# Chunks 6 and 7 of a retention layer computed in halves of 64 tokens, with their k and v loaded head by head

## The chip, the core and the metric

One core of one Trainium2 chip runs the whole program in a single launch. The core has a matrix engine (TensorE, "PE" in the profile, whose weight loads are listed apart as "PEld"), a vector engine (VectorE, "DVE"), a scalar engine (ScalarE, "ACT"), GpSimd ("POOL") and SyncE ("SP"). In this kernel SP issues every DMA, one after the other, from one queue. The metric is the device time of one execution in microseconds; lower is better.

## The reference

Two layers follow each other. The first is a recurrent retention over q, k and v of shape (4 batches, 8 heads, 768 tokens, 64); the second is a feed-forward layer with a squared ReLU over the 4 x 768 = 3072 tokens of width 512.

```python
gamma = 1.0 - 2.0 ** (-5.0 - np.arange(H))
scale = 1.0 / np.sqrt(D)
for t in range(S):
    state = gamma[None, :, None, None] * state + np.einsum('bhd,bhe->bhde', k[:, :, t], v[:, :, t])
    y[:, :, t] = scale * np.einsum('bhd,bhde->bhe', q[:, :, t], state)
...
x = y.transpose(0, 2, 1, 3).reshape(B * S, H * D)
h = np.maximum(x @ w_in, 0.0)      # w_in: 512 x 2048
out = h * h @ w_out                # w_out: 2048 x 512
```

## The kernel before

**Chunks.** The tokens are cut into 24 chunks of 128 (six for each batch): chunks 0 to 5 are batch 0, 6 to 11 batch 1, and so on. In a chunk the recurrence is replaced by matrix products: scores of q against k, masked to the causal half, times v, plus q times the state that the chunks before have left. The powers of gamma are multiplied into q and k beforehand. Heads are taken in four pairs.

**Three ways to compute a chunk.** Chunks 0 to 3 are done in pairs before the main loop (`..._pair` functions). From there on there are two ways, and `PACK_FROM` (L25) says where the second begins:

- Whole chunks (`attend`, L916): `scale_q` and `scale_kv` (DVE for q and k, POOL for v) make bf16 copies, `transpose_q` (L360) and `transpose_k` (L374) transpose them on PE, `scores` (L396) multiplies 128 tokens by 128 tokens, `state` (L420) adds k times v to the state in PSUM (`c_ps`) and copies it to a block-diagonal SBUF tile (`s_bd`), and `outputs` (L465) makes `y` and copies it to `xt`, the input of the feed-forward layer. q, k and v come by `load_q` (L84, 512 KB for two chunks) and `load_kv` (L102, 256 KB for k and 256 KB for v of one chunk).
- Halves of 64 tokens (`attend2`, L928): the two heads of a pair stand on the two halves of the partitions. `scale_k2` (L618, DVE, two instructions), `cast_v2` (L631, POOL: a plain copy `v2` and two instructions for the block-diagonal `v_bd`), `transpose_k2` (L642) and `dma_transpose_q` (L388), which transpose by DMA, `scores2` (L651), `state2` (L678, once for each half; its result goes to `s_bd` first on ACT, L697, and then on DVE, L698), `outputs2` (L700; its copy to `xt` on ACT is L724). k and v come by `batch_loads` (L120): eight DMAs for each part of a batch, one for each head, each of them 64 partitions wide. The tile that they fill comes from the `stage` pool, which the weights have used before.

**Feed-forward.** `BLOCKS` (L18) groups the chunks: block 0 has chunks 0 to 3, each block after it has two. `ffn_pieces` (L786) yields after every piece of PE work. A piece is 16 products with `w_in` (L757, 128 columns) or four with `w_out` (L815, 512 columns) around here. Block 1 (chunks 4 and 5) has pieces 33 to 48: 33 to 40 the first product, 33 to 36 of chunk 4 and 37 to 40 of chunk 5, 41 to 48 the second. Block 2 (chunks 6 and 7) has pieces 49 to 64 in the same way: 49 to 52 need `xt` of chunk 6, 53 to 56 that of chunk 7. Block 3 (chunks 8 and 9) begins with piece 65.

**Order of the work.** There is no scheduler. `put(place, ...)` writes by hand after which piece each step of the attention is issued, and every engine takes its instructions in that order. A place therefore fixes the order on each engine and in SP's queue, not a time: an engine that has nothing to wait for runs ahead of PE. `done` (L961) is the place of `outputs2` for each chunk done by halves, and `attend2` puts the chunk's `state2` and `scores2` at fixed distances ahead of it. `places` (L971) spreads the single DMAs of `batch_loads`.

Lines that matter most here:

```python
put(max(d - 6, before), state2, m, 0)
put(d - 5, scores2, m)
put(d - 3, state2, m, 1)
put(d, outputs2, m)
```

## Time and profile before

| | |
|---|---|
| median of 3 runs | 213.44 us (213.25 to 213.58) |
| the profiled execution | 215.1 us, its core's span 213.3 us |
| granted TensorE clock, mean | 0.998 |
| DVE, ACT and POOL busy | 63%, 55% and 27% of the span |
| DMA moved | 40.18 MB in 92,727 packets, 68,512 of them under 512 B |
| L757 and L815, the feed-forward products | 90.6 us and 89.6 us of PE's busy time |
| L132, a load of 128 KB | 8 for k, 5.8 us from issue to landing; 8 for v, 5.1 us |
| L108, a load of 256 KB | 4 for k, 6.1 us; 4 for v, 6.5 us |
| L645, transposition of k by DMA | 16, 3.8 us |
| L391, transposition of q by DMA | 8, 3.4 us |

The profile is one execution. An engine's busy time is a union of its instructions; PE's matmuls are pipelined and overlap, so the distance from one start to the next is the better measure of what a matmul costs. A wait is put down to the last semaphore that it needed. Positions such as "at 60.72 us" are counted from the start of the span.

### The profile page before, as it was taken

The page shows a single profiled execution, that of the slowest core. Times are in us where ns is not written, and L with a number is a line of the kernel's source. Part 1 is how long each engine was busy: PE and PEld are TensorE (multiplying, and loading weights), DVE is VectorE, ACT ScalarE, POOL GpSimd, SP SyncE. Part 2 cuts the span into 40 slices and gives each one's busy share as a digit, 9 for nine tenths or more (in the row PEclk, how much of TensorE's full clock was granted, in tenths as well). Part 3 has the DMA queues.
Part 4 walks back from the last instruction along what each step waited for, and adds up shares of the span by engine and source line. Part 5 has one row for each costly group of instructions (what it writes and reads, how often), then busy time and mean ns, then how long its engine had stood idle before and what let it go on. Part 6 is the DMA issues. An engine that isn't in the chain of part 4 may idle for free.

```text
span 213.3 us, 5243 instructions
## 1 busy us (share of the span) xinstructions
PE 205.2 (96%) x2117; PEld 141.4 (66%) x2117; DVE 134.7 (63%) x263; ACT 117.0 (55%) x220; POOL 57.9 (27%) x114
## 2 busy tenths in 40 slices
PE   5798999999999999999999999999999999999994
PEld 1467744457965984884875875874965965965853
DVE  4677787235798997396495596595694793640410
ACT  8345887158953763662663663652753754643631
POOL 5232458223102523142230343052130433000000
PEclk9999999999999999999999999999999999999999
DMA  5999999999999997969978998959988451701102
GB/s 163 292 318 383 383 384 252 285 242 293 247 160 175 259 167 140 254 111 231 189 124 152 271 166 205 242 105 190 239 150 211 103 98 49 101 0 52 49 0 98
DMA packets 92727, 40.18 MB, mean 188 GB/s; under 512 B 68512, under 2 KB 86176, under 8 KB 92704
## 3 DMA queue, kind: packets, MB, share of 16 engines
q1 hardware_dynamic: 92704, 39.86, 83.1%
q8 instruction: 16, 0.26, 0.5%
q14 instruction: 7, 0.06, 0.1%
HBM read 27.26 MB, written 6.29 MB: 157 GB/s over the span
## 4 chain that ended last, share of the span: by engine, by line
PE 78%; DVE 8%; SPq 5%; DMA 4%; ACT 3%; issue 1%; ACTq 0%; DVEq 0%
PE psf L815 34%; PE psf L757 33%; SPq L132 4%; DMA kn<-in_k_dram 3%; DVE ks_bdp L623 2%; DVE h L737 2%; DMA stage<-in_v_dram 2%; PE y L717 2%; PE y L710 2%; PE st L661 2%; PE c_ps L688 1%; PE y L316 1%; PE c_ps L565 1%; DVE pt L548 1%; PE psf L524 1%
## 5 line engine op out<-in xcount | busy, mean ns | idle before, releaser
L757 PE MATMUL psf<-xt,w_in_bf 128*128 128x256 bf16 (+2 forms) x880 | 90.6, 259 | 0.2 <-ACT xt L488 0.2
L815 PE MATMUL psf<-w_out_bf,h 128*128 128x512 bf16 (+2 forms) x400 | 89.6, 371 | 0.0
L757 PEld LDWEIGHTS <-w_in_bf 128*128 128x128 bf16 x880 | 71.1, 98 | 11.6 <-issue 0.3
L766 ACT ACTIVATE h<-psf 128x512 bf16<-128x512 f32 x96 | 57.1, 597 | 22.2 <-PE psf L757 19.4
L815 PEld LDWEIGHTS <-h 128*128 128x128 bf16 x400 | 36.0, 98 | 35.7 <-DVE h L737 1.0
L737 DVE TENSOR_TENSOR h<-h 128x512 bf16<-128x512 bf16 x96 | 45.1, 492 | 17.8 <-ACT h L766 17.2
L698 DVE CAST s_bd<-c_ps 64x256 bf16<-64x256 f32 x29 | 12.4, 427 | 31.1 <-ACT s_bd L697 30.8
L637 POOL CAST v_bd<-stage 64x512 bf16<-64x512 f32 x32 | 23.2, 726 | 28.1 <-PE y L717 27.1
L825 ACT ACTIVATE osb<-psf 128x512 f32<-128x512 f32 (+2 forms) x25 | 14.5, 580 | 28.8 <-PE psf L815 28.8
L634 POOL CAST v<-stage 128x512 bf16<-128x512 f32 x16 | 11.3, 705 | 61.7 <-DMA stage<-in_v_dram 28.8
L623 DVE TENSOR_TENSOR ks_bdp<-stage,kf 64x512 bf16<-64x512 f32 x32 | 24.9, 779 | 0.6
L724 ACT ACTIVATE xt<-y 128x512 bf16<-128x512 f32 x16 | 11.9, 741 | 13.5 <-PE y L717 13.5
L335 DVE TENSOR_TENSOR qs<-qn,qf 128x512 bf16<-128x512 f32 x22 | 15.4, 709 | 2.3 <-DMA qn<-in_q_dram 2.0
L697 ACT ACTIVATE s_bd<-c_ps 64x256 bf16<-64x256 f32 x29 | 10.6, 367 | 10.3 <-PE c_ps L688 8.1
L411 DVE TENSOR_TENSOR pt<-st,cmask 128x512 bf16<-128x512 f32 x8 | 5.5, 689 | 10.1 <-PE st L404 10.1
L668 DVE TENSOR_TENSOR pt<-st,cmask 128x512 bf16<-128x512 f32 x16 | 11.1, 691 | 0.5
L304 POOL CAST w_out_bf<-stage 128x512 bf16<-128x512 f32 x12 | 8.3, 724 | 5.3 <-DMA stage<-in_moe_w_out_dram 5.3
L688 PEld LDWEIGHTS <-ks_bdp 128*128 128x128 bf16 x116 | 7.2, 98 | 3.4 <-issue 0.4
L717 PE MATMUL y<-pt,v_bd 128*128 128x64 bf16 x128 | 9.4, 193 | 0.0
L710 PE MATMUL y<-qT,s_bd 128*128 128x64 bf16 x120 | 9.1, 193 | 0.0
L710 PEld LDWEIGHTS <-s_bd 128*128 128x128 bf16 x120 | 8.2, 98 | 1.1
L717 PEld LDWEIGHTS <-v_bd 128*128 128x128 bf16 x128 | 8.1, 98 | 1.2
(99 smaller groups left out, 141.9 us busy)
## 6 DMA issues: line engine op xcount, KB each, us to landing
qn<-in_q_dram SPq DMA_DIRECT2D x12, 512.0 KB, 5.0
out_dram<-osb SPq DMA_DIRECT2D x23, 256.0 KB, 3.8
stage<-in_moe_w_out_dram SPq DMA_DIRECT2D x4, 1024.0 KB, 8.0
stage<-in_moe_w_in_dram SPq DMA_DIRECT2D x3, 1024.0 KB, 11.7
stage<-in_k_dram SPq DMA_DIRECT2D x32, 96.0 KB, 3.6
stage<-in_v_dram SPq DMA_DIRECT2D x32, 96.0 KB, 3.3
kn<-in_k_dram SPq DMA_DIRECT2D x2, 512.0 KB, 6.8
vn<-in_v_dram SPq DMA_DIRECT2D x2, 512.0 KB, 7.5
```

The source lines that it names most:

```text
L335: engine.tensor_tensor(out=out, in0=by, in1=table[:, :, None].to_broadcast([P, H, D]), op=ALU.mult)
L623: nc.vector.tensor_tensor(out=ks[rows, :, hh, :].rearrange("s (u p) d -> s u p d", u=2), in0=kn[rows], in1=kf2[rows, i, :, :, None].to_bro ...
L637: nc.gpsimd.tensor_copy(v_bd[rows, :, hh, :].rearrange("s (u p) d -> s u p d", u=2), vn[rows])
L698: nc.vector.tensor_copy(s_bd[halves[1], :, 1, :], c[halves[1]])
L710: nc.tensor.matmul(yv, lhsT=s_bds[(2 * m + u - 1) % 3][:, p], rhs=half_of(a["qT"], p, u), start=True, stop=False,)
L717: nc.tensor.matmul(yv, lhsT=a["v_bd"][:, u * NPAIR + p], rhs=a["pt"][:, u * NPAIR + p, :].rearrange("s (r t) -> s r t", r=2), start=not inter,
L724: nc.scalar.activation(xts[tb][:, :, off : off + C].rearrange("e p (s r) -> e p r s", r=2), y[:], AF.Copy,)
L737: nc.vector.tensor_mul(hv, hv, hv)
L757: nc.tensor.matmul(hp, lhsT=w_in_bf[g][:, cb, fq * 128 : (fq + 1) * 128], rhs=xts[tb][:, cb, cols], start=(cb == 0), stop=(cb == NCB - 1),)
L766: nc.scalar.activation(hv, hp[:], AF.Relu)
L815: nc.tensor.matmul(op[:], lhsT=h_of(tb, f)[:, 0, j * C : (j + 1) * C], rhs=w_out_bf[g][:, fq, cols], start=(f == 0), stop=(f == NFB - 1),)
L825: nc.scalar.activation(osb[:, cols], op[:], AF.Copy)
```

## The change

`PACK_FROM` goes from 8 to 6, so chunks 6 and 7 are computed in halves too. What follows from it:

- Their k and v are no longer loaded by `load_kv`. `batch_loads` now takes a list of widths: for batch 1 `[2, 4]`, that is eight DMAs of 64 KB for chunks 6 and 7 and eight of 128 KB for chunks 8 to 11; for the other batches `[3, 3]` as before. k of 6 and 7 is issued at places 13 and 14. v of 6 and 7 is issued at places 31, 32, 35 and 36, two at each. The DMA that transposes q of chunks 6 and 7 is put at place 31 and that of k of chunk 6 at place 34. k and v of 8 to 11 move from places 30 to 37 to places 38 to 45.
- `outputs2` of chunks 6, 7, 8 and 9 stands at places 47, 52, 59 and 63 (before: `outputs` of 6 and 7 at 42 and 49, `outputs2` of 8 and 9 at 57 and 62).
- The constants and the zeroing for the halves are made earlier. The loads of q for 6 and 8 move by one place, and those of batch 2 by two or three.
- `state` serves chunk 4 alone now, and loses its form for the batches after the first.

```diff
-PACK_FROM = 8
+PACK_FROM = 6
...
-        for w in range(0, NCH - i, size):
+        for w, size in zip(np.cumsum([0] + sizes).tolist(), sizes):
...
-    for m, place in ((5, 10), (6, 14), (7, 18)):
-        put(place, load, m)
+    put(10, load, 5)
+    put(13, load_q, 6)
...
-    attend(6, 30, (33, 35, 37, 39, 42))
-    attend(7, None, (40, 42, 44, 46, 49))
-    put(34, pack_constants)
-    for j, t in enumerate([s_bds[2]] + ks_bd2s + v_bd2s):
+    put(24, pack_constants)
+    for t, place in zip(ks_bd2s + [s_bds[2]] + v_bd2s, (22, 24, 26, 34, 36)):
         for hh in range(2):
-            put(35 + 2 * j + hh, zero_off_diagonal, t, hh)
-
-    put(29, load_q, 8)
+            put(place + hh, zero_off_diagonal, t, hh)
+
+    put(30, load_q, 8)
     put(41, load_q, 10)
-    done = [57, 62] + [70 + 8 * j for j in range(14)]
+    done = [47, 52, 59, 63] + [70 + 8 * j for j in range(14)]
 
     ahead = {
-        8: (36, 40, 44, 46, 48), 9: (0, 0, 49, 51, 53), 10: (50, 54, 55, 57, 58), 11: (0, 0, 60, 63, 63)
+        6: (29, 31, 33, 34, 41), 7: (0, 0, 36, 38, 44), 8: (42, 45, 48, 50, 49), 9: (0, 0, 52, 54, 54),
+        10: (50, 55, 57, 59, 60), 11: (0, 0, 61, 63, 64),
     }
...
     places = {
-        (8, "k"): [30 + j // 2 for j in range(8)],
-        (8, "v"): [34 + j // 2 for j in range(8)],
-        (12, "k"): [47, 48, 49, 50, 52, 53, 55, 56] + [74 + j for j in range(8)],
-        (12, "v"): [58, 59, 60, 61, 62, 64, 65, 66] + [82 + j for j in range(8)],
+        (6, "k"): [13 + j // 4 for j in range(8)] + [38 + j // 2 for j in range(8)],
+        (6, "v"): [31, 31, 32, 32, 35, 35, 36, 36] + [42 + j // 2 for j in range(8)],
+        (12, "k"): [50, 51, 53, 54, 55, 56, 57, 58] + [74 + j for j in range(8)],
+        (12, "v"): [60, 61, 62, 64, 65, 66, 67, 68] + [82 + j for j in range(8)],
...
-        loads = batch_loads(m, name, 4 if m == 8 else 3)
+        loads = batch_loads(m, name, [2, 4] if m == 6 else [3, 3])
```

In `ahead` the five numbers are the places of `scale_q`, `dma_transpose_q`, `scale_k2`, `transpose_k2` and `cast_v2`. The instructions as built: PE has eight matmuls fewer (2111 instead of 2119, branches counted), SP 15 DMAs more, POOL four casts more, DVE two instructions more, ACT three fewer. In SP's queue the order around the change is: q of 6 and 7, the eight k loads of 6 and 7, two stores of results, q of 8, a third store, the transposition of q of 6 and 7, two v loads, the fourth store, two v loads, the transposition of k of 6, four v loads, the transposition of k of 7, six k loads of 8 to 11, q of 10, two k loads, four v loads, a store, two v loads, the transposition of q of 8 and 9, two v loads.

More of the change, by code (lines that the diff above doesn't have):

```diff
@@ L118, in stage_tile, with batch_loads @@
         return t[:, 0:size]
-    def batch_loads(m, name, size):
+    def batch_loads(m, name, sizes):
         b, i = chunks[m]
@@ L426, in state @@
         if i == 0:
-            c_ps[0] = ps_c.tile([P, NPAIR, D], FP32, name="c_ps")
+            c_ps[0] = ps_c.tile([P, NPAIR, 2, D], FP32, name="c_ps")
         c = c_ps[0]
-        if b == 0:
-            for p in range(NPAIR):
-                nc.tensor.matmul(
-                    c[:, p],
-                    lhsT=a["ks"][:, 2 * p : 2 * p + 2, :],
-                    rhs=a["v_bd"][:, p, ::3, :],
-                    start=False,
-                    stop=True,
-                    skip_group_check=True,
-                )
-        else:
-            for p in range(NPAIR):
-                for hh, head in enumerate(halves):
-                    nc.tensor.matmul(
-                        c[head, p, :],
-                        lhsT=a["ks"][:, 2 * p + hh, :],
-                        rhs=a["v_bd"][:, p, 3 * hh, :],
-                        start=(i == 0 and p == 0),
-                        stop=True,
-                        skip_group_check=True,
-                    )
-        s_bd = s_bds[(2 * m + 1) % 3]
-        for hh, head in enumerate(halves):
-            of = c[head, :, hh, :] if b == 0 else c[head]
+        for p in range(NPAIR):
+            nc.tensor.matmul(
+                c[:, p],
+                lhsT=a["ks"][:, 2 * p : 2 * p + 2, :],
+                rhs=a["v_bd"][:, p, ::3, :],
+                start=(i == 0 and p == 0),
+                stop=True,
+                skip_group_check=True,
+            )
+        s_bd = s_bds[m % 2]
+        for hh in range(2):
+            rows = slice(64 * hh, 64 * (hh + 1))
             if hh < on_scalar:
-                nc.scalar.activation(s_bd[head, :, hh, :], of, AF.Copy)
+                nc.scalar.activation(s_bd[rows, :, hh, :], c[rows, :, hh, :], AF.Copy)
             else:
-                nc.vector.tensor_copy(s_bd[head, :, hh, :], of)
+                nc.vector.tensor_copy(s_bd[rows, :, hh, :], c[rows, :, hh, :])
     def xt_of(m):
@@ L473, in outputs @@
                     y[:, p, :],
-                    lhsT=s_bds[(2 * m - 1) % 3][:, p],
+                    lhsT=s_bds[(m - 1) % 2][:, p],
                     rhs=a["qT"][:, :, p, :],
```

## The prediction

> **What bounds the kernel now.** I read the page first (busy time, chain), then PE's timeline and SP's, then the landings of DMAs and the casts on POOL.

> ```profile
> PE 205.2 (96%) x2117; PEld 141.4 (66%) x2117; DVE 134.7 (63%) x263; ACT 117.0 (55%) x220; POOL 57.9 (27%) x114
> ```

> PE is busy for 205.2 of 213.3 us. Of the 8.1 us idle most lies in the first 20 us (PE busy for 15.5 of them) and in the last 13; between 30 and 200 us the timeline has three waits, of 0.19, 0.18 and 0.14 us. So the time is PE's work, and nearly every new wait of PE is added to it. PE's timeline where the change works, columns start, length, instruction, count:

> ```profile
> 59.82 1.07 PE L757 MATMUL psf<-xt,w_in_bf 128*128 128x128 bf16 x16
> 60.72 1.89 PE L815 MATMUL psf<-w_out_bf,h 128*128 128x512 bf16 x8
> 62.45 0.61 PE L480 MATMUL y<-pt,v_bd 128*128 128x128 bf16 x8
> 63.24 0.40 PE L378 MATMUL tp<-ident,ks 128*128 128x128 bf16 x4 [0.18 <-DVE ks L335]
> ...
> 79.06 0.28 PE L688 MATMUL c_ps<-v,ks_bdp 128*128 128x64 bf16 x4
> 79.18 0.40 PE L661 MATMUL st<-qT,kT 128*128 128x64 bf16 x8
> 79.41 1.89 PE L815 MATMUL psf<-w_out_bf,h 128*128 128x512 bf16 x8
> 81.44 0.28 PE L688 MATMUL c_ps<-v,ks_bdp 128*128 128x64 bf16 x4
> ```

> The reader takes start-to-start distances: a piece of 16 L757 costs 0.90 us, a piece of four L815 0.865 us, and place 40 is at 60.72. SP's queue is the other thing to see:

> ```profile
> 50.90 0.57 SPq L827 DMA_DIRECT2D out_dram<-osb  x1
> 51.52 1.30 SPq L132 DMA_DIRECT2D stage<-in_k_dram  x2
> 52.92 0.68 SPq L827 DMA_DIRECT2D out_dram<-osb  x1
> 53.65 3.60 SPq L132 DMA_DIRECT2D stage<-in_k_dram  x4
> 57.34 6.71 SPq L132 DMA_DIRECT2D stage<-in_v_dram  x8
> 64.16 1.70 SPq L391 DMA_TRANSPOSE qT<-qs  x1
> ```

> From 49 to 66 us SP issues without a gap, and one load takes it 0.63 us at least (median 0.65 for these eight v loads, some up to 1.4). What hangs on it:

> ```profile
> 67.71 0.89 POOL L634 CAST v<-stage 128x512 bf16<-128x512 f32 x1 [11.42 <-DMA stage<-in_v_dram]
> ```

> POOL has waited 11.42 us for the last of these loads. Today that is harmless: `state2` of chunk 8 needs this cast at 72.80 only.

> **PE's work.** Removed, by distances in PE's timeline: transposition of q of 6 and 7 0.45 (eight at 52.33); of k 0.22 and 0.23; scores with state 0.22 + 0.56 for each chunk (59.26 to 59.82 holds four scores and eight state products); outputs 0.79 for chunk 6 (62.45 to 63.24, the wait of 0.18 with it) and 0.67 for chunk 7. Sum 3.92 us. Added, from the same operations on later chunks: four states of 0.12, two scores of 0.23, outputs 0.46 (78.60 to 79.06) and 0.35 for a batch's first chunk (107.82 to 108.17). Sum 1.75. Net **-2.17 us**. A wait for `xt` of chunk 5 takes back 0.1, since only piece 36 is left between its `outputs` and piece 37. On DVE, ACT and POOL the differences hide: PE waits for none of their sums, only at the points below.

> **Hand-over of chunk 7 (B).** `outputs2` of chunk 7 is at place 52 and piece 53 reads its `xt` at once; before, three pieces lay between. After chunk 8's last output at 79.06 ACT starts the copy at 79.26 and takes 0.75, so PE stands still for **1.0 us** (up to 1.6 if a ReLU of 0.60 is ahead on ACT; not below 0.9, there is nothing to cover it).

> **State of chunk 9 (C).** Its two `state2` are now at places 59 and 60 with one piece between, 0.12 + 0.865 = 0.98 us from start to start. The second overwrites the PSUM that ACT and DVE copy, behind chunk 8's copy to `xt`. In the lines above the same pair is 2.38 us apart, of it the wait of 0.14. DVE came 0.7 us late there, behind squares of h; without them it would be 1.7. So PE waits 0.7 to 1.4; I take **1.1**, less today's 0.14.

> **v of chunk 6 (D).** `state2` of chunk 6 at place 41 needs `cast_v2`, and that all eight v loads. When does PE come? 60.72 less what is removed ahead of it (0.45 + 0.22 + 0.22 + 0.56 = 1.45), plus 0.1, plus piece 41: **60.2**. When does v come? Until the third store PE and SP run as now, so it issues at 50.90, when ACT has its result, and ends at 51.5. Then SP issues in turn, each with 0.04 between: transposition of q 1.32 (the q copy on DVE was done by 49.6), two loads 1.34, a store 0.6, two loads 1.34, transposition of k 1.3, three loads 2.0. The eighth starts at 59.5. From issue to landing v loads take

> ```profile
> stage<-in_v_dram SPq DMA_DIRECT2D x32, 96.0 KB, 3.3
> stage<-in_v_dram SPq DMA_DIRECT2D x8, 128.0 KB, 5.1
> ```

> No row has 64 KB. From below: 2.6, the shortest of any load between 45 and 110 us; from above: 5.1. I take 3.3, the nearest size. POOL started 0.3 after the landing (the load issued at 63.42 landed 4.0 later) and casts in 0.66 to 0.89: v2 is there at 63.8, from 62.8 (2.6 + 0.66 and no delay) to 65.8. PE waits **3.6 us** (2.6 to 5.6). Moving the k loads of 6 and 7 to places 13 and 14 costs nothing: eight of 0.67 take the 5.1 us that four loads take now (41.42 to 46.53), ahead of the first store at 47.54. Behind the waiting state stand all of PE's later pieces.

> [...] Here v of 6 and 7 costs SP 2.26 us now (1.25 at 42.45, 1.01 at 45.52) and 5.4 then. [...]

> **v of chunks 8 to 11 (E).** It stands behind all that: from 59.5, the eighth load 0.67, transposition of k of 7 1.33, six k loads 4.0, q 0.62, two k 1.34, four v 2.7, a store 0.6, two v 1.34, transposition of q 1.37, one v 0.67. The last load starts at 74.2, against 63.42 now. It lands 4.0 later, as the last one does now; POOL 0.3 and 0.89: **79.4**. From below (2.6 and 0.66): 77.5. From above: the twelve loads from 53.65 to 64.05 took 0.87 each, 0.2 more than 0.67; for 15 loads 3.0, so 82.4. PE comes to place 53 at 63.8 + 13.3 = 77.1. The 13.3 are the pieces 42 to 53, 0.865 or 0.894 each, 10.5 us; four states, two scores and two outputs, 1.75; and B. So PE waits another 2.3.

> **Sum.** From place 53 on, the run of before takes 213.3 - 74.93 = 138.4 us (74.93 is where piece 53 ends now, 73.81 + 0.23 + 0.89). Then come 0.35 for the state and score of chunk 8, which lay ahead of it, and C's 0.96: 139.7. 79.4 + 139.7 = 219.1 us of span. By terms: 213.3 - 2.17 + 0.1 + 3.6 + 1.0 + 2.3 + 0.96 = 219.1. The profiled execution's own time is 215.1 and its span 213.3; the median of the runs, 213.44, lies 0.14 above that span, so I predict **219.2 us**.

> **Rivals.**
> 1. Only v of 6 is late; SP's later loads land in time (E = 0). For it: in the stage from 69.5 the loads of 96 KB already took 3.3. Against it: fifteen loads, three more issues than now and the chain from the third store stand ahead of the last one. 77.1 + 139.7 = 216.8, so 216.9 us; with D at its lower end 215.9.
> 2. The other side, not slower: SP's queue keeps ahead of PE. It decides at 59.2 us, when the eighth load would have to have landed, and at 72.5 for the last one of chunks 8 to 11. Then place 53 is at 60.2 + 13.3 = 73.5, and 213.2 + 0.14 = 213.3 us; with B at 0.9 and C at 0.7, 212.8. For it: SP waits for nothing of PE but stores, and the DMAs have 0.5 MB less to fetch between 41 and 47 us. Against it: the third store ties the queue to ACT at 50.90, and the ten issues between it and the eighth load take 8.0 us.
> 3. The DMA engines are the bound, and loads come at 0.87: place 53 at 82.4, 222.2 us. For it: the DMA share is 9 of 10 or more from 20 to 70 us. Against it: that stage now holds fewer bytes.

> That the change doesn't do what it says is excluded by the order of the built instructions.

> **How the numbers follow.** Forecast 0.60 (its own range 217.2 to 221); rival 1 0.18; rival 3 0.14; rival 2 0.08. The range from 215.8 to 222.4 leaves out rival 2 and parts of the others' tails, some 0.17. About 0.2% is what a measurement of this kernel can tell from no change, so of rival 2's 0.08 half is within it and half faster (212.8 and less); all else is slower: 0.92.

> **What would show it.** PE waits at L688's `c_ps` for POOL's v2 cast near 60 and near 77 us, some 3.6 and 2.3 long; one of 1.0 for ACT's `xt` just ahead, near 75; one of about 1 for DVE's `s_bd` near 87. SP issues without a gap from 49 to 75, with the last v load of chunk 8 at 74. L757 and L815 keep their busy time. I am wrong if PE's waits between 55 and 90 us sum to under 4 us, if the waits name a kT or ks_bdp instead of v2, or if v loads land under 2 us.

## The result, and the profile after

The changed kernel takes 226.1 us (median of 4 runs, 224.63 to 226.69) where the kernel before takes 213.34 on the same chip: a ratio of 1.0577, 95% interval 1.0546 to 1.0608. It is slower, as forecast, but by 12.8 us instead of 5.8, and it lies above the range. The profiled execution took 226.39 us, its span 224.6.

First PE's busy time and granted clock (the 40 slices are 5.6 us each):

```profile
PE 206.2 (92%) x2087; PEld 142.4 (63%) x2109; DVE 133.6 (59%) x265; ACT 114.5 (51%) x217; POOL 59.3 (26%) x118
...
PEclk9999999999979976999999999999999999999999
```

and the clock row of before:

```profile
PEclk9999999999999999999999999999999999999999
```

PE has less to do and is still busy a microsecond longer. The clock row says why: in three slices, 62 to 67 and 79 to 90 us, the clock fell; in the profile of before it is at half only from 212.44 us on, behind PE's last product. PE's timeline shows where (start, length, instruction, count, and in brackets the wait ahead of it with what ended it):

```profile
63.85 0.28 PE L675 MATMUL c_ps<-v,ks_bdp 128*128 128x64 bf16 x4 [4.30 <-POOL v L621]
63.97 1.75 PE L802 MATMUL psf<-w_out_bf,h 128*128 128x512 bf16 x4
65.51 0.64 PE L648 MATMUL st<-qT,kT 128*128 128x64 bf16 x8
...
77.90 1.05 PE L744 MATMUL psf<-xt,w_in_bf 128*128 128x128 bf16 x16 [0.85 <-ACT xt L711]
83.19 0.37 PE L675 MATMUL c_ps<-v,ks_bdp 128*128 128x64 bf16 x4 [4.23 <-POOL v L621]
83.37 1.90 PE L744 MATMUL psf<-xt,w_in_bf 128*128 128x128 bf16 x16
...
93.57 0.28 PE L675 MATMUL c_ps<-v,ks_bdp 128*128 128x64 bf16 x4 [0.54 <-DVE s_bd L685]
```

All four waits that the forecast named are there, at the instructions and for the releasers that it named: D 4.30, B 0.85, E 4.23, C 0.54. These are idle times; from start to start, as the forecast counted, they are 4.46, 1.02, 4.40 and 0.70. (The lines are those of before less 13: L675 was L688, L621 was L634.) Behind D four products with `w_out` take 1.54 us from start to start, 63.97 to 65.51, where before they took 0.865. Behind E a piece of 16 products with `w_in` takes 1.69, 83.37 to 85.06, instead of 0.89. SP's queue, in which v comes:

```profile
51.01 2.41 SPq L391 DMA_TRANSPOSE qT<-qs  x1
53.51 1.27 SPq L132 DMA_DIRECT2D stage<-in_v_dram  x2
...
58.45 2.60 SPq L132 DMA_DIRECT2D stage<-in_v_dram  x4
61.16 1.26 SPq L632 DMA_TRANSPOSE kT<-ks_bdp  x1
62.46 4.64 SPq L132 DMA_DIRECT2D stage<-in_k_dram  x6
...
69.21 4.04 SPq L132 DMA_DIRECT2D stage<-in_v_dram  x4
...
77.49 2.38 SPq L132 DMA_DIRECT2D stage<-in_v_dram  x2
```

The eighth load of v of 6 and 7 starts at 60.43 (forecast 59.5), the last of v of 8 to 11 at 79.23 (forecast 74.2, before 63.42). Four 128 KB loads that were to take 2.7 us take 4.04, two take 2.38. POOL answers with its casts:

```profile
63.19 0.61 POOL L621 CAST v<-stage 128x512 bf16<-128x512 f32 x1 [17.63 <-DMA stage<-in_v_dram]
...
82.52 0.61 POOL L621 CAST v<-stage 128x512 bf16<-128x512 f32 x1 [15.60 <-DMA stage<-in_v_dram]
```

**Where the 11.3 us of span come from.** I compare both traces between two instructions that both have, the 65th product with `w_in` and the 400th from the last. That stretch takes 83.93 us before and 96.05 after, 12.12 more; ahead of it the profiled execution of before is 0.84 slower, behind it both are alike. The gaps between PE's instructions sum to 0.50 before and 10.58 after: +10.08. The rest is work, 83.42 and 85.47. In an execution without loads of v and of the later k (`no_kv_loads` below, clock 1.00) the same work takes 81.89. So PE's own work fell by 1.53, and the fallen clock added 85.47 - 81.89 = 3.58. -1.53 + 10.08 + 3.58 = 12.13.

What the DMAs did meanwhile, as busy time by stretch (PE, PEld, DVE, ACT and POOL with their counts, then the granted clock; the last two numbers are the busy share of the 16 DMA engines and GB/s), before:

```profile
42.00:53.00 11.00, 10.81 (x101) 6.92 (x100) 4.86 (x8) 6.97 (x14) 4.20 (x18) 1.00 1.25 265
53.00:63.00 10.00, 10.00 (x159) 8.80 (x156) 8.22 (x22) 7.23 (x13) 0.76 (x1) 1.00 1.14 212
63.00:73.00 10.00, 9.82 (x112) 6.79 (x111) 8.76 (x16) 5.33 (x9) 4.72 (x6) 1.00 1.10 222
```

and after:

```profile
42.00:53.00 11.00, 10.76 (x111) 7.39 (x111) 6.01 (x10) 7.05 (x13) 2.34 (x4) 1.00 0.81 190
53.00:63.00 10.00, 6.50 (x103) 5.85 (x102) 6.08 (x15) 4.52 (x8) 0.00 (x0) 1.00 0.98 195
63.00:73.00 10.00, 9.10 (x72) 4.75 (x73) 3.04 (x6) 2.22 (x6) 3.55 (x6) 0.83 0.92 183
73.00:83.00 10.00, 5.10 (x99) 4.89 (x96) 6.54 (x13) 4.45 (x8) 0.48 (x1) 0.91 1.19 188
```

From 42 to 73 us the DMAs move 265 x 11 + 212 x 10 + 222 x 10 = 7.3 MB before and 5.9 MB after. A queue that issues one load of 64 KB in 0.66 us feeds 99 GB/s; the 1.4 MB that are missing come later, when the engines are busier again (share 1.19).

### The profile page after: what moved, and what is told of

The parts are those of the page before. It is cut to its first block, busy times and chain, and to the rows that moved or that the text cites. A ratio compares the mean times of both kernels' runs of the same rounds, so it can differ in the third digit from the quotient of the medians.

```text
span 224.6 us, 5233 instructions
## 1 busy us (share of the span) xinstructions
PE 206.2 (92%) x2087; PEld 142.4 (63%) x2109; DVE 133.6 (59%) x265; ACT 114.5 (51%) x217; POOL 59.3 (26%) x118
## 2 busy tenths in 40 slices
DMA packets 96087, 40.96 MB, mean 182 GB/s; under 512 B 71872, under 2 KB 89536, under 8 KB 96064
## 4 chain that ended last, share of the span: by engine, by line
PE 82%; DMA 5%; DVE 4%; ACT 2%; issue 2%; SPq 2%; POOL 1%; POOLq 0%; DVEq 0%; ACTq 0%
PE psf L802 35%; PE psf L744 34%; DMA stage<-in_v_dram 2%; DMA kn<-in_k_dram 2%; PE st L648 2%; PE c_ps L675 2%; PE y L704 2%; PE y L697 2%; SPq L132 2%; DVE ks_bdp L610 1%; DVE h L724 1%; PE y L316 1%; DVE pt L535 1%; PE psf L511 1%; PE c_ps L552 1%
## 5 line engine op out<-in xcount | busy, mean ns | idle before, releaser
L744 PE MATMUL psf<-xt,w_in_bf 128*128 128x256 bf16 (+2 forms) x879 | 92.4, 263 | 1.1 <-ACT xt L711 0.9
L744 PEld LDWEIGHTS <-w_in_bf 128*128 128x128 bf16 x880 | 73.1, 100 | 12.6 <-issue 1.3
L685 DVE CAST s_bd<-c_ps 64x256 bf16<-64x256 f32 x33 | 14.1, 428 | 45.2 <-ACT s_bd L684 44.9
L621 POOL CAST v<-stage 128x512 bf16<-128x512 f32 x18 | 12.1, 671 | 81.7 <-DMA stage<-in_v_dram 64.8
L624 POOL CAST v_bd<-stage 64x512 bf16<-64x512 f32 x36 | 25.7, 714 | 27.1 <-PE y L704 26.0
L610 DVE TENSOR_TENSOR ks_bdp<-stage,kf 64x512 bf16<-64x512 f32 x36 | 27.0, 749 | 0.7
L711 ACT ACTIVATE xt<-y 128x512 bf16<-128x512 f32 x18 | 13.3, 742 | 18.6 <-PE y L704 18.6
L684 ACT ACTIVATE s_bd<-c_ps 64x256 bf16<-64x256 f32 x33 | 12.1, 367 | 18.0 <-PE c_ps L675 15.8
L675 PE MATMUL c_ps<-v,ks_bdp 128*128 128x64 bf16 x132 | 9.3, 194 | 9.1 <-POOL v L621 8.5
L335 DVE TENSOR_TENSOR qs<-qn,qf 128x512 bf16<-128x512 f32 x22 | 15.6, 723 | 2.9 <-DMA qn<-in_q_dram 2.7
L675 PEld LDWEIGHTS <-ks_bdp 128*128 128x128 bf16 x132 | 8.2, 98 | 13.2 <-issue 10.0
L655 DVE TENSOR_TENSOR pt<-st,cmask 128x512 bf16<-128x512 f32 x18 | 12.5, 692 | 2.1 <-POOL v_bd L624 1.2
L704 PE MATMUL y<-pt,v_bd 128*128 128x64 bf16 x144 | 10.6, 193 | 0.0
```

The lines of the kernel that those rows point to most:

```text
L335: engine.tensor_tensor(out=out, in0=by, in1=table[:, :, None].to_broadcast([P, H, D]), op=ALU.mult)
L610: nc.vector.tensor_tensor(out=ks[rows, :, hh, :].rearrange("s (u p) d -> s u p d", u=2), in0=kn[rows], in1=kf2[rows, i, :, :, None].to_bro ...
L624: nc.gpsimd.tensor_copy(v_bd[rows, :, hh, :].rearrange("s (u p) d -> s u p d", u=2), vn[rows])
L675: nc.tensor.matmul(c[:, p, :], lhsT=a["ks"][:, u * NPAIR + p], rhs=a["v2"][:, u * NPAIR + p, :], start=(i == 0 and u == 0 and p == 0), sto ...
L685: nc.vector.tensor_copy(s_bd[halves[1], :, 1, :], c[halves[1]])
L704: nc.tensor.matmul(yv, lhsT=a["v_bd"][:, u * NPAIR + p], rhs=a["pt"][:, u * NPAIR + p, :].rearrange("s (r t) -> s r t", r=2), start=not inter,
```

## The experiments

Sixteen kernels, in four groups. Each was timed against the kernel before on the same chip (213.47 to 213.71 us). Intervals are of the ratio. All start from the changed kernel. Positions in two profiles differ by up to 0.9 us before the change has any effect (see the last section), so lengths say more than positions.

### Does the fallen clock cost what the trace says?

`filled`: 18 idle products with the identity are issued ahead of the `state2` at place 41, and 26 ahead of the one at place 53.

```diff
+    def fill(n):
+        keep_awake(n, pool=ps_tp, name="tp")
+        end_awake()
+
+    put(41, fill, 18)
+    put(53, fill, 26)
```

> Idle matmuls (identity, results unused) stand in PE's queue ahead of the two states that wait for v2: 18 of 0.216 us at place 41 and 26 at place 53. Nothing else changes. Theory (a wait of some 4 us costs once more afterwards, by PE's halved clock): matmuls behind both waits run at full speed; what the first one gives back (1.7) is swallowed by the second, which ends at the same time, and what the second gives back (2.3) stays: about 223.8 us, granted clock near 0.998. Rival 'the clock has nothing to do with the waits': 226.1 and the clock still at 0.97.

Measured 223.52 us, 1.0463 (1.0408 to 1.0518). Busy time by stretch (the third number from the end is the granted clock), `filled`:

```profile
60.00:70.00 10.00, 9.22 (x77) 4.78 (x77) 3.33 (x5) 1.78 (x4) 3.90 (x6) 1.00 0.81 175
80.00:90.00 10.00, 9.84 (x118) 6.49 (x118) 5.76 (x11) 3.42 (x8) 5.26 (x9) 1.00 1.02 167
```

and the changed kernel:

```profile
60.00:70.00 10.00, 6.15 (x35) 2.89 (x35) 2.75 (x5) 1.24 (x3) 3.55 (x6) 0.83 0.71 152
80.00:90.00 10.00, 6.76 (x70) 6.10 (x71) 3.15 (x6) 2.43 (x5) 4.36 (x7) 0.66 0.88 187
```

With PE kept busy the clock stays at 1.00 in both stretches (0.83 and 0.66 without) and 2.6 us come back, as the theory had it. That is less than 3.58: what is saved behind D is spent until v of 8 comes, whose cast starts only 0.3 us sooner, counted from the 65th product with `w_in` (58.82 us behind it instead of 59.12).

### Is v late because of the number of issues or because of the bytes?

`half_bytes`: the loads of k and v of 8 to 11 carry 64 KB instead of 128 KB.

```diff
-            to[m + j] = t[:, :, 2 * j : 2 * j + 2]...
+            at_j = j - 2 if m == 6 and j >= 4 else j
+            to[m + j] = t[:, :, 2 * at_j : 2 * at_j + 2]...
-        loads = batch_loads(m, name, [2, 4] if m == 6 else [3, 3])
+        loads = batch_loads(m, name, [2, 2] if m == 6 else [3, 3])
```

> The loads of k and v for chunks 8 to 11 carry half of their bytes (chunks 8 and 9 only; chunks 10 and 11 are computed from the k and v of 8 and 9), with as many DMAs in the same order. Theory 'SP needs 0.63 us for each issue whatever its size': the last v load is issued near 79 as now, about 225.5 us. Rival 'the DMA engines are full and SP's issues wait for them': the issues of 0.8 to 1.7 us fall to 0.63, which is 3.6 us in all, and landings come 2 us sooner; about 221 to 222 us. I expect between the two: 223.

Measured 221.34 us, 1.0355 (1.0319 to 1.0391). At the same number of issues the last v load starts at 75.08 instead of 79.23 and lands at 77.46 instead of 82.37; no wait for v of 8 is left, but one of 1.16 for kT of 8. Some 0.9 of this is only an earlier start of the execution. The length tells more: from the eighth v load of 6 and 7 to the last of 8 to 11 SP takes 15.62 us instead of 18.80, and the four v loads in a row need 2.59 instead of 4.04:

```profile
68.19 2.59 SPq L133 DMA_DIRECT2D stage<-in_v_dram  x4
```

That is the rival's outcome. So it is mostly by their bytes that v of 8 to 11 came late: four issues take 2.59 instead of 4.04, the last two 1.27 instead of 2.38. The six k loads in a row did not get shorter (4.68 us, in the changed kernel 4.64).

`v67_half`: the eight v loads of 6 and 7 alone carry half (widths `[1, 4]` for v).

> The eight v loads of chunks 6 and 7 carry 32 KB instead of 64 KB, the others what they carry in the changed kernel (v of chunk 7 is that of chunk 6, v of 8 to 11 is that of 7 to 10; the output differs). Theory (issue-bound: SP issues one load per 0.65 us, and the engines have landed it before the next four are out): eighth load issued at 60.4 as before, wait at place 41 3.7 to 4.3 us, 225.3 to 226.3 us. Rival (byte-bound): the issues ahead of it get shorter and the wait falls below 3.3 us; 225 us or less.

Measured 224.58 us, 1.0522 (1.0483 to 1.0562), which its interval doesn't separate from the changed kernel. D is 2.68 and the time is under 225, both as the rival had them, but the rival's reason is not there: six of the loads take SP 0.60 or 0.61 us, as in the changed kernel (the others 0.96 and 1.16), and from the first of the eight to the last it takes 7.49 us, with 6.92 in the changed kernel. The eighth lands 2.03 us after its issue instead of 2.46. The rest is that SP came to k of 6 and 7 at 41.45 us in this execution and at 42.87 in the one of after, so that the eighth load started 1.34 sooner. E took back what D lost: 6.62. That the spacing of these eight loads comes from issues and not from bytes rests on those lengths, not on the time; D's size changes by over a microsecond from one execution to the next. Behind this wait the clock did not fall (1.00 from 63 to 73 us), and four products with `w_out` take 0.86 us:

```profile
62.08 0.28 PE L676 MATMUL c_ps<-v,ks_bdp 128*128 128x64 bf16 x4 [2.68 <-POOL v L622]
62.19 1.03 PE L803 MATMUL psf<-w_out_bf,h 128*128 128x512 bf16 x4
63.05 0.40 PE L649 MATMUL st<-qT,kT 128*128 128x64 bf16 x8
```

`two_early`: v of 6 and 7 put at places 15 and 16, straight behind their k and ahead of the stores.

```diff
-        (6, "v"): [31, 31, 32, 32, 35, 35, 36, 36] + [42 + j // 2 for j in range(8)],
+        (6, "v"): [15, 15, 15, 15, 16, 16, 16, 16] + [42 + j // 2 for j in range(8)],
```

> The loads of the changed kernel in size and number; only v of 6 and 7 is put at places 15 and 16, ahead of the stores. It tells the order of the issues from their number. Theory (the wait for v of 8 swallows the one for v of 6, since as many issues lie ahead of its last load): no wait at place 41 and no fall of the clock there, the wait at place 53 grows from 4.2 to 8 us, 226.1 - 1.7 = 224.4 us (223.5 to 225.5). Rival (each wait on its own): 226.1 - 4.3 - 1.7 = 220 us.

Measured 225.06 us, 1.0521 (1.0494 to 1.0549). The time is the theory's, the way is not. v of 6 is early, but the transposition of q of 6 now starts at 56.93 instead of 51.01 and kT of 6 at 59.78 instead of 57.11; PE waits 3.15 us for kT one step later, the clock falls there (0.83 from 60 to 70 us), and E stays at 4.60. In both kernels PE waits for what SP issues last for chunk 6.

`six_at_once`: 16 loads of 192 KB for all six chunks instead of 32 of 64 and 128 KB.

```diff
-        (6, "k"): [13 + j // 4 for j in range(8)] + [38 + j // 2 for j in range(8)],
-        (6, "v"): [31, 31, 32, 32, 35, 35, 36, 36] + [42 + j // 2 for j in range(8)],
+        (6, "k"): [13 + j // 4 for j in range(8)],
+        (6, "v"): [15 + j // 4 for j in range(8)],
...
-        loads = batch_loads(m, name, [2, 4] if m == 6 else [3, 3])
+        loads = batch_loads(m, name, [6] if m == 6 else [3, 3])
```

> k and v of chunks 6 to 11 in eight loads each (192 KB instead of 64 KB and 128 KB), k's at places 13 and 14 and v's at 15 and 16, ahead of the stores; PE's order is the changed kernel's. Theory (it is the sixteen further issues in SP's queue): 16 x 0.65 = 10.4 us of SP go, v of 6 is there by 58 to 61 us (PE comes at 59.6), that of 8 with it; the waits of 0.85 and 0.54 stay: 213.5 - 2.17 + 0.1 + 0.85 + 0.4 and 0 to 1.5 for v of 6, 212.6 to 214.2 us, no fall of the clock. Rival (the bytes ahead are the bound): 3.1 MB of k and v and 1 MB of stores and q from 41.5 us at 190 GB/s end at 63 us, so v of 6 is awaited for 4 us with a fall of the clock behind it, but no other: 218 to 219 us.

Measured 227.79 us, 1.0663 (1.0646 to 1.068): slower than the changed kernel. SP's queue:

```profile
41.41 9.79 SPq L132 DMA_DIRECT2D stage<-in_k_dram  x8
51.32 10.22 SPq L132 DMA_DIRECT2D stage<-in_v_dram  x8
```

Sixteen issues take 20 us, 1.25 each, and not 0.65: the loads land 1.21 us apart (47.36 to 65.55 for fifteen), 162 GB/s, and SP's issues go at that pace. v of 6 now comes with the bytes of five other chunks, PE waits 7.24 us for it and 3.04 for kT of 6. The theory that the number of issues alone is at fault falls here. The rival's size was also too small: it put v of 6 at 63 us, its cast began at 65.93.

`six_v_later` (the same loads, v at places 31 to 36) and `six_bc` (`six_at_once` with `done` at 46, 51, 58, 64 and `cast_v2` of 6 a place earlier):

> The same eight loads of 192 KB each, with v's where the changed kernel has v of 6 and 7 (places 31 to 36, between stores and transpositions). Theory: the eighth is issued at 60.4 us as in the changed kernel, and lands 4 to 5 later instead of 2.5: the wait at place 41 is 6 to 7 us with 2 us of fallen clock behind it, the one for v of 8 is gone: 213.5 - 2.17 + 0.1 + 0.85 + 0.4 + 6.5 + 2 = 221 us (219.5 to 222.5). Rival (only the count of issues matters, not the order): as in the kernel with v ahead of the stores, within 1 us.

> As the first of these, and chunks 6 to 9 end at places 46, 51, 58 and 64 instead of 47, 52, 59 and 63, so that a piece more lies between the outputs of chunk 7 and the first reader of its xt and between the states of chunk 9. Theory (with no wait for v left, these two add up): the waits of 0.85 and 0.54 go, 1.3 us less than the first, 211.3 to 213 us and so below the kernel before. Rival (v of 6, now awaited a piece sooner, takes it back): a wait of up to 1 us more at place 40 and a time within 0.5 of the first.

`six_v_later` 230.05 us, 1.0769 (1.0734 to 1.0804), with one wait of 14.33 us for v of 6: both its theory and its rival missed. `six_bc` 229.97 us, 1.075 (1.0705 to 1.0795), with waits of 8.21, 2.93 and 1.97, 2.2 us slower than `six_at_once`: here too neither came true. What was to be gained behind the loads never showed, as they still were the bound.

### Does another queue help?

Here `batch_loads` issues some of batch 1's v loads by `nc.scalar` (ScalarE) or `nc.gpsimd` (GpSimd) instead of `nc.sync`, and their places move (in the changed kernel the first eight, v of 6 and 7, stand at 31 to 36, the other eight at 42 to 45):

| kernel | issued by | first eight at | other eight at |
|---|---|---|---|
| `v67_on_act` | ScalarE, the others SP | 18 to 21 | 42 to 45 |
| `v_on_act` | ScalarE, all | 18 to 21 | 24 to 28 |
| `v_act_late` | ScalarE, all | 27 to 30 | 38 to 41 |
| `v_on_pool` | GpSimd, all | 27 to 30 | 38 to 41 |
| `v67_on_pool` | GpSimd, the others SP | 27 to 30 | 42 to 45 |

The edit of the first of them, shortened:

```diff
-                    nc.sync.dma_start(
+                    (nc.scalar if (m, name, w) == (6, "v", 0) else nc.sync).dma_start(
...
-        (6, "v"): [31, 31, 32, 32, 35, 35, 36, 36] + [42 + j // 2 for j in range(8)],
+        (6, "v"): [18, 18, 19, 19, 20, 20, 21, 21] + [42 + j // 2 for j in range(8)],
```

> The eight v loads of chunks 6 and 7 are issued by ACT at places 18 to 21, where it is idle, instead of by SP. Theory (SP's queue sets both waits for v2): the wait near 60 us (4.30) goes and with it the slow matmuls behind it; SP comes to the k loads of chunks 8 to 11 about 4.1 us sooner, because the transposition of k of chunk 7 then waits for DVE at 57.1 and ends at 58.4 instead of 62.5; the second wait ends at about 79 instead of 83.2. PE reaches it at 73 and waits some 6 us. Time about 222.0 us. Rival 'the two waits add up': 226.1 - 4.3 - 1.7 = 220.1. Rival 'the DMA engines, not the issuing, set the landing of v': the second wait still ends near 83, 226 us.

> All sixteen v loads of batch 1 are issued by ACT at places 18 to 28. Theory (SP's queue): both waits for v2 go; what is left of the change is -2.17 of matmuls, 0.85 for the hand-over of chunk 7 and 0.54 for chunk 9's state: about 212.5 to 213.6 us, as before the change. Rival 'DMA engines': v lands by 70, but k of 8 to 11 or the transpositions take the place, 217 us or more. Rival 'ACT becomes the bound': ReLUs behind the issues hold back PE between 36 and 50 us by up to 16 x 0.65 = 10 us.

`v67_on_act` 234.32 us, 1.0955 (1.0894 to 1.1017); `v_on_act` 228.23 us, 1.0693 (1.0647 to 1.0739). In both D is gone, in the second E too (it is 6.59 in the first), and ScalarE has become the bound. That is the last of the three forecasts for `v_on_act`; none of those for `v67_on_act` came true. ScalarE's timeline in `v_on_act`:

```profile
36.45 12.84 ACTq L132 DMA_DIRECT2D stage<-in_v_dram  x6
49.34 0.63 ACT L306 ACTIVATE w_out_bf<-stage 128x512 bf16<-128x512 f32 x1 [14.84 <-issue]
```

and what PE waits for:

```profile
50.02 0.58 PE L802 MATMUL psf<-w_out_bf,h 128*128 128x512 bf16 x1 [8.67 <-ACT w_out_bf L306]
```

Six issues hold ScalarE for 12.84 us, and a cast of weights behind them is late. Here issuing wasn't free of the engine's compute: ScalarE had computed nothing for 14.84 us when the cast began.

> The same sixteen loads at the same places, issued by ScalarE. Theory (in the two runs before, ScalarE stood at loads that had been put ahead of its last cast of w_out and of q's copy; behind them it has the time): its sixteen issues of 0.63 us are 10 us, ScalarE's idle time from 43 to 60 us is some 8, so xt and the ReLUs come up to 2 us late: 213 to 216 us, with PE waiting for ScalarE once or twice for under 1 us. Rival (any queue of loads blocks the engine that issues it while the DMA engines are full): a wait of 3 us or more for ScalarE, 218 us or more.

226.38 us, 1.06 (1.0548 to 1.0651): the rival. Moved behind the cast, the loads hold ScalarE further on, two of them for 6.27 us:

```profile
63.12 6.27 ACTq L132 DMA_DIRECT2D stage<-in_v_dram  x2
69.44 0.60 ACT L753 ACTIVATE h<-psf 128x512 bf16<-128x512 f32 x1 [5.75 <-DMA stage<-in_v_dram]
```

At 72.31 PE has waited 5.00 us for the copies of the state, of which ScalarE makes one.

> All sixteen v loads of chunks 6 to 11 issued by GpSimd, which stood idle from 45.6 to 63.2 us, from place 27 on, behind its last cast of w_out. Theory (it was the order of issues in one queue, not the bytes): v of 6 is there by 55 to 58 us and that of 8 by 65 to 70, both waits and the two falls of the clock gone; 212.5 to 214 us. Rival 1 (the bytes are the bound; the loads fill the DMA engines wherever they are issued): k, kT or v still late by 2 to 4 us, 216 to 220 us. Rival 2 (GpSimd issues slowly or keeps DVE waiting): v of 6 later than 60 us or DVE's operations longer, 217 us or more.

230.45 us, 1.0792 (1.0757 to 1.0828). GpSimd issues evenly, at 0.61 to 0.69 us, and v is no longer awaited. But everything in flight slows down. From issue to landing v of 128 KB takes 5.1 us in the changed kernel, k of 128 KB 4.4, a store 3.8, the transposition of k 3.2, all from 45 to 75 us; here k takes 6.7, a store 5.7, and:

```profile
stage<-in_v_dram POOLq DMA_DIRECT2D x8, 128.0 KB, 14.4
...
kT<-ks_bdp SPq DMA_TRANSPOSE x2, 16.3
```

kT of 6 comes 18.6 us after its issue and PE waits 12.82 us for it. Rival 1 had k or kT late by 2 to 4 us, and it had the bytes as the reason; but from 60 to 70 us the DMAs move 123 GB/s with a busy share of 1.12, against 184 GB/s at 1.09 in the kernel before. Engines that are as busy and move a third less are not a matter of bytes alone.

> Only the eight v loads of chunks 6 and 7 issued by GpSimd, from place 27 on; those of 8 to 11 stay on SP where they are. Theory: SP's queue is eight issues (5.3 us) shorter ahead of v of chunk 8; the wait for v of 6 is gone, the last v load of 8 is issued at 74 and cast at 77.5 to 78.5, while PE comes to place 53 at 74: a wait of 4 us there with 2 of fallen clock: 213.6 - 2.17 + 0.1 + 0.85 + 0.4 + 4 + 2 = 218.8 us (217.5 to 220). Rival (loads from two queues clog the engines as in the run with all sixteen on GpSimd): qT or kT of 6 lands 10 us or more after its issue, a wait of 4 us or more at the scores of 6, 222 us or more.

222.23 us, 1.0424 (1.037 to 1.0478), the fastest of this group. D is gone and q's transposition lands 7.7 us after its issue, so the rival's clog is not there. But E is 8.31 (forecast 4), in a profiled execution of 224.12 us, the slowest of the four. SP is rid of eight issues, 5.3 us, and its last v load starts at 76.92 instead of 79.23, 2.3 sooner. The rest is taken back by longer issues (the transposition of q of 8 and 9 takes 3.91). In the stretch compared above this execution takes 93.44 us and the one of the changed kernel 96.05: the gaps fell from 10.58 to 9.94, since v of 8 came earlier, and the work from 85.47 to 83.50, since the clock falls once instead of twice. What more the medians differ by, 3.9 us in all, no profile shows.

### What is left when nothing is loaded?

`bc_undone`: `done = [47, 51, 58, 63]`.

> Outputs of chunk 7 at place 51 and of chunk 8 at place 58, so that each has a piece more behind it. Theory (the wait for v of chunk 8 takes whatever is gained ahead of it, since that v comes by SP's queue and not by PE): the wait of 0.85 us for xt of chunk 7 goes and the one of 4.23 for v of chunk 8 grows by as much; only the 0.54 for s_bd of chunk 9, behind it, is gained: 225.6 us. Rival (the four waits add up, each on its own): 0.85 + 0.54 less, 224.7 us.

225.42 us, 1.0571 (1.0523 to 1.0618). B is gone and E is 5.22, 4.23 + 0.85 = 5.08 being expected. C is gone too, but the two states of chunk 7 are now a piece apart and cost the same 0.53 at 72.35. The interval doesn't separate it from the changed kernel.

`no_v_loads`: no v loads for chunks 6 to 11; `cast_v2` reads k's tile.

> The sixteen v loads of chunks 6 to 11 are left out and their casts read k's staged tile (the output differs). Theory (everything above the time of before comes from SP's late v; PE's own work did shrink by 2.17): no wait for v, none over 0.5 us for kT, clock 1.0 throughout, 213.3 - 2.17 + 0.1 + 0.85 + 0.4 = 212.5 us (211.8 to 213.5). Rival 1 (the saving in PE's work was misjudged, or the clock falls for another reason): 214 or more without waits over 1 us. Rival 2 (kT is nearly as late as v and takes its place): waits of 1 to 3 us at the scores of chunk 6 or 8, 215 to 218 us.

217.2 us, 1.0173 (1.0148 to 1.0198). Rival 2, smaller than it said: kT of 8, 9 and 10 is late by 0.83, 0.81 and 1.08, and one `s_bd` by 1.20. k of 8 to 11, issued from 58.5 us now and from 49.3 before, stands in SP's queue behind the transposition of k of 7, which starts at 57.20.

`no_kv_loads`: k of 8 to 11 isn't loaded either, but read from the tile of 6 and 7.

> Of chunks 6 to 11 only k of 6 and 7 is loaded; k of 8 to 11 is read from that tile and v from k's tile (the output differs). Theory (PE's own saving is there, and all else that was lost came from loads in SP's queue): no wait for v or kT over 0.3 us; B's 0.85 and C's 0.54 stay; 213.6 - 2.17 + 0.1 + 0.85 + 0.4 = 212.8 us (212 to 213.5). Rival (the new order of work on DVE and ACT costs PE as much as the loads did not): waits for s_bd, kT or pt of together 3 us or more, 215.5 us or more.

214.08 us (10 runs), 1.0011 (0.9993 to 1.003): as the kernel before, 1.3 us above the theory and below the rival. The waits are those expected and one more, and the clock is 1.00:

```profile
50.36 1.05 PE L747 MATMUL psf<-xt,w_in_bf 128*128 128x128 bf16 x16 [0.19 <-ACT xt L476]
71.74 1.05 PE L747 MATMUL psf<-xt,w_in_bf 128*128 128x128 bf16 x16 [0.85 <-ACT xt L714]
80.94 0.28 PE L678 MATMUL c_ps<-v,ks_bdp 128*128 128x64 bf16 x4 [0.53 <-DVE s_bd L688]
86.72 0.41 PE L651 MATMUL st<-qT,kT 128*128 128x64 bf16 x8 [0.57 <-DMA kT<-ks_bdp]
```

2.14 us of waits against 0.51 before: 1.63 more, which is what PE's smaller work (1.53) saves.

`no_kv_bc`: the same with `done = [46, 51, 58, 64]` and `cast_v2` of 6 a place earlier.

> As the run without loads of v and without k of chunks 8 to 11 (the output differs), and chunks 6 to 9 end at places 46, 51, 58 and 64 instead of 47, 52, 59 and 63. Theory (PE's own work fell by 1.5 us by the traces, and the waits of 0.85 and 0.54 took it back): both waits go and none over 0.6 comes, 214.1 - 1.4 = 212.7 us (212.2 to 213.2). Rival (another wait takes their place, so that the saving never shows): 213.6 us or more.

215.55 us (9 runs, 214.14 to 217.01), 1.008 (1.0046 to 1.0114): the rival. In the profiled execution, with 216.51 us one of the slower, B and C are gone and kT of chunk 8, needed a piece sooner, is late:

```profile
73.72 0.61 PE L651 MATMUL st<-qT,kT 128*128 128x64 bf16 x8 [2.24 <-DMA kT<-ks_bdp]
74.13 3.36 PE L747 MATMUL psf<-xt,w_in_bf 128*128 128x128 bf16 x32
```

Behind this wait, too, the clock fell (0.83 from 70 to 80 us): 32 products in 3.20 us from start to start (74.13 to 77.33) instead of 1.79. No version that I ran beats the kernel before, and even without the loads the saving never showed.

## Why the prediction was right and wrong

**What bounds the kernel, the direction, and the four waits** were right: places, releasers and order as forecast, 10.6 us in sum from start to start where the terms gave 8.0 (3.6 + 1.0 + 2.3 + 1.1). B measured 1.02 (forecast 1.0), C 0.70 (1.1, its lower end 0.7: DVE was not behind squares this time).

**D** was right in mechanism and came out at 4.46 instead of 3.6. v2 was ready at 63.80, where 63.8 was forecast, and that was luck: the eighth load started 0.93 later, because the transposition of q took SP 2.41 us and not 1.32, but it landed 2.46 after its issue and not 3.3, and the cast took 0.61 and not 0.89. The wait grew because PE came 0.8 sooner, as this execution runs 0.84 ahead of the one of before that the forecast counted from. That these eight loads are spaced by SP's issues and not by their bytes is what the lengths in `v67_half` show (7.49 us from the first to the last at half the bytes, 6.92 at full); where the 1.1 us more for the transposition of q come from stays open.

**E is the step that failed.** "The last load starts at 74.2" prices fifteen loads at 0.67 each, as if SP were free to issue. It started at 79.23. From the eighth load on the forecast allowed 14.7 us; it took 18.80, and 15.62 with half the bytes, so 3.2 of the 4.1 us that were missing go with the bytes. In its place stands what the third rival said: the DMA engines bound these loads (`half_bytes`, `six_at_once`, `v67_on_pool`). That rival put place 53 at 82.4; it was at 83.19, or 84.0 on the clock of the execution that the forecast counted from. I gave it 0.14 because "that stage now holds fewer bytes" than before, a reading of one stage. The bytes hadn't gone: by the rows above they had been pushed back behind a stretch in which loads of 64 KB left the engines short (190 and 195 GB/s from 42 to 63 us, before 265 and 212).

**The clock was missing from the sum.** The line "L757 and L815 keep their busy time" was wrong; 3.58 us came from matmuls at the fallen clock behind D and E. That a long wait costs more than itself stood in no term and no rival. In the changed kernel the granted clock stood at 0.50 for 3.41 us from 64.12, behind D, and for 6.83 us from 81.19, behind E. The length of a wait alone doesn't decide. In the clock records of all 18 traces the granted clock changes only on a grid of 3.41 us (in the changed kernel it is at 1.00 and 0.50 in turn for 51.20, 3.41, 13.65, 6.83 and 136.53 us). Between 33 and 120 us every step of that grid in which PE was idle for 2.22 us or more in sum (the least in `no_kv_bc`, a wait of 2.24) was followed by half speed, and none with 1.70 or less (the most in `six_bc`, the first part of its wait of 8.21) was. The wait of 2.68 us in `v67_half` was cut by the grid into 1.00 and 1.68, and the clock stayed at 1.00.

**PE's work** was put at -2.17 and measured -1.53. The attention's products fell by 1.82 (11.69 to 9.87 us in the stretch compared above, before and `no_kv_loads`); the products with `w_in` took 0.41 more and those with `w_out` 0.13 less, which I can't explain.

**The span and the median.** "The median of the runs, 213.44, lies 0.14 above that span" took the profiled execution for a typical one. It was a slow one: others of the kernel before have spans of 211.2 to 212.5 at times of 213.01 to 214.29, some 1.8 less than their time. So the base was a span some 1.6 us too long, and what was added to it some 1.6 too short. For an execution that starts like the others of before the two errors cancel; the profiled one of the changed kernel starts only 0.84 ahead of the profile of before, so about half of the second error is left.

Together: 219.2 + 4.6 (v2 of 8 at 83.2 instead of 79.4, in an execution that runs 0.84 ahead) + 1.7 (behind place 53, 141.4 instead of 139.7: the clock behind E, less C) + 0.8 (1.65 of the step from span to time, less 0.84) = 226.3; the profiled execution took 226.39. What D and its clock added ahead of place 53 is in none of these terms, because the wait for v of 8 swallowed it, as `two_early`, `v67_half` and `bc_undone` show.

Fewer and larger loads were no remedy: in `six_at_once`, loads of 192 KB halved the issues and cost 1.7 us more. Nor did a second queue give back all that it took off SP: in `v67_on_pool` SP had 5.3 us of issues less, and its last v load started 2.3 us sooner.

## What to carry to other kernels

When PE is the bound, price an edit of the loads as a queue with two limits, issues (here 0.65 us each) and bytes (here 162 GB/s in `six_at_once`, 183 to 188 between 63 and 83 us of the changed kernel, 71,872 of 96,087 packets under 512 B), and follow the bytes that are put off into the next stage. A wait of PE can cost a second time, through the clock; here it did when at least 2.22 us of idle time fell into one step of 3.41. A saving of PE's work is only there if the hand-overs around it keep their distance: here 1.53 us of work were paid with 1.63 us of waits even when nothing was loaded.
